# Normalising the last two chunks of V as steps of their own, behind the second pair's masks, in an attention, gMLP and GLU kernel

## The chip, the cores and the metric

The kernel runs on one core of a Trainium2 chip. The metric is the device time of one execution, in microseconds (us). Times below are from the profiler's trace of one execution unless they are called the median.

## The reference

Three blocks follow one another, for a batch of 4 sequences of 576 positions. All arrays are float32.

```python
# 1 attention: 8 heads of 64, causal, window of 128, ALiBi bias
attn = softmax(where(mask, q @ k.T / 8 + bias, -1e9));  x = heads_joined(attn @ v)
# 2 gMLP: d_model 512, d_ff 1024
h = gelu_tanh(x @ w_in);  u, v = h[..., :512], h[..., 512:]
v_n = (v - mean(v)) / sqrt(var(v) + 1e-6) * g_ln
x2 = x + (u * (einsum('ts,bsd->btd', w_sg, v_n) + b_sg)) @ w_out
# 3 GLU: width-3 convolution over positions
h2 = relu(x2 @ w_in2);  out = (h2 * sigmoid(conv3(h2, conv_w))) @ w_out2
```

The change concerns `v_n` of the first sequence (batch 0): the mean and the variance of each position's 512 values of v, and the normalised rows that the product with `w_sg` needs over all 576 positions.

## The kernel before

Every matrix product of blocks 2 and 3 is made of three float32r products (high part times high part, high times low, low times high), so every operand is split into a high and a low part: a copy that rounds (`hi`, L246) and a subtraction of it from the source (`lo`, L249).

The work is a list of steps, written out in `_steps` (L54 to L121) and run in that order by `run` (L889). A letter names the step and numbers its batch and tile. C is a head pair's scores on TensorE (PE) and its nine masked row maxima on VectorE (DVE), L451; E its nine exponentials on ScalarE (ACT), L493; N the reciprocal of the sums (L498, L499) and the nine scalings by it, on GpSimd (POOL) or DVE (L242); T its transposes; A the product with the attention's v, out of which an x tile comes. V is one chunk of 128 positions of the gMLP's v (chunk 4 has 64): 12 matmuls into `psv`, Gelu on ACT, mean and variance on DVE (L781, L782), the reciprocal root on POOL (L784, L785), the normalisation on DVE (L786) and its split, high part on ACT, low part on DVE (L787). U is one tile of u, G one of the product with `w_sg` (14 matmuls into `pss`, evicted by DVE at L843, then multiplied by u on POOL at L821 and split, which is the gate), W one of the product with `w_out` (`pso`). L and M load a pair's k, q and v; g and o load and split a piece of `w_sg` and `w_out`, the last with five DVE instructions (L324 to L331), a copy on ACT and a subtraction on POOL.

A scheduler turns the list into one fixed order for each engine: it takes instructions by readiness in a time model and, among the ready ones, by their place in the list. At run time each engine then keeps its order. `add_manual_dep` with `follow` puts one instruction behind another in that order, and adds no semaphore. All of `act`'s activations keep the list's order among themselves (L188). `pick` (L204) chooses an engine for some copies by booked loads; `book` adds to those loads.

In batch 0 the V, U, g and o steps are mixed with the scores of batch 1 (line 93 and 94 of `_steps`): V0.4 and V0.3 stand ahead of C1.1, the scores of batch 1's second pair; then come U0.1.2, U0.1.3 and C1.2, then E1.0, N1.0 and the four tiles G0.0.0 to G0.0.3. A G tile reads the normalised chunks in the order 0, 1, 2, 3, 4 (L834), three matmuls for each of the first four and two for the last. The scores have six PSUM banks (L276), and one pair takes five of them, which its masks give back.

Of the kernel before, what the change touches and what calls it, by code (L numbers as in the profile page):

```python
# [7 lines left out]
F32 = mybir.dt.float32  # L8
# [3 lines left out]
AF = mybir.ActivationFunctionType  # L12
ALU = mybir.AluOpType

B, H, S, D = 4, 8, 576, 64
P = 128
DM = H * D
FF = 1024
HF = FF // 2
# [12 lines left out]
NV = 3  # L32
# [21 lines left out]
def _steps():  # L54


    def of(p):
        return f"{p // NP}.{p % NP}"

    def scores(p):  # L60
        return [f"C{of(p)}"]

    def weigh(p):
        return [f"E{of(p)}", f"N{of(p)}"]

    def back(p):
        return [f"T{of(p)}", f"A{of(p)}"]

    def halves(p):
        return [f"X{of(p)}.0", f"X{of(p)}.1"]  # L70

    def loads(p):
        return [f"L{of(p)}", f"M{of(p)}"]

    weave = lambda main, more: [
        x for i, m in enumerate(main) for x in [m] + more[i * len(more) // len(main) : (i + 1) * len(more) // len(main)]
    ]
    put_by = [f"a{i}.{c}" for i in (1, 0) for c in range(16)]
    s = """
        l0.0 k0 l1.0 k5 l2.0 l3.0 v0.0 v1.0 v2.0 v3.0 j1.0 j1.1 l0.1  # L80
        c0.0 e0.0 c1.0 e1.0 n0.0 c2.0 e2.0 t0.0 n1.0 c3.0 e3.0 l1.1 j1.2 j1.3 v0.1 i1.0 z0.0 X0.0.0 t1.0 n2.0 z1.0 X0.1.0
        l2.1 v1.1 i1.1 t2.0 n3.0 z2.0 X0.2.0 c0.1 e0.1 l3.1 j0.0 i1.2 t3.0 z3.0 X0.3.0 c1.1 e1.1 v2.1 i1.3 n0.1 c2.1 j0.1 v3.1 j0.2 t0.1 e2.1 n1.1 z0.1
        i0.0 c3.1 e3.1 j0.3 i0.1 k4 V0.0 t1.1 n2.1 z1.1 V0.1 t2.1 n3.1 z2.1 i0.2 U0.0.0 i0.3 t3.1 z3.1 X0.0.1 U0.0.1
        X0.1.1 U0.0.2 X0.2.1 X0.3.1
    """.split()
    for b in range(B - 1):
        p = NP * (b + 1)
        V = [f"V{b}.{j}" for j in range(5)]
        U = [[f"U{b}.{half}.{m}" for m in range(4)] for half in range(2)]
        G = [[f"G{b}.{half}.{m}" for m in range(4)] for half in range(2)]  # L90
        W = [[f"W{b}.{half}.{m}" for m in range(4)] for half in range(2)]
        if b == 0:
            uv = ["g0", "g1", V[2], "g2", "o0.0", U[0][3], "g3", "o0.1", V[4]] + loads(p) + ["g4", "o1.0"] + scores(p) + ["o1.1", V[3], "o2.0", "o2.1"]
            uv += loads(p + 1) + U[1][:2] + ["o3.0"] + scores(p + 1) + ["o3.1"] + loads(p + 2) + U[1][2:] + scores(p + 2)
        else:
            uv = V[:2] + loads(p) + scores(p) + V[2:] + loads(p + 1) + scores(p + 1) + U[0] + loads(p + 2) + U[1][:1] + scores(p + 2) + U[1][1:]
        T, A = ([f"{x}{of(p + i)}" for i in range(4)] for x in "TA")
        gw = weigh(p) + G[0] + weigh(p + 1) + G[1][:1] + loads(p + 3) + T[:1] + G[1][1:2] + W[0][:1] + A[:1] + halves(p)
        gw += weigh(p + 2) + W[0][1:2] + T[1:2] + W[0][2:] + A[1:2] + scores(p + 3) + halves(p + 1) + weigh(p + 3) + T[2:3] + G[1][2:3]
        gw += A[2:3] + halves(p + 2) + G[1][3:] + T[3:] + W[1][:1] + A[3:] + halves(p + 3) + W[1][1:]  # L100
        if b == 0:
            s += uv + gw
        else:
            now = put_by[10 * b - 10 : 10 * b]
            s += ["B1"] + weave(uv, now[:4]) + ["B0"] + weave(gw, now[4:])
    first = " ".join(s)
    n = [f"V3.{j}" for j in (0, 1, 2, 4, 3)] + [f"U3.{half}.{m}" for half in range(2) for m in range(4)]
    n += [f"G3.0.{m}" for m in range(4)] + ["G3.1.0"] + [f"W3.0.{m}" for m in range(4)]
    n += [f"G3.1.{m}" for m in range(1, 4)] + [f"W3.1.{m}" for m in range(4)]

    for m in range(4):
        n[n.index(f"U3.{m % 2}.{m // 2 + 1}")] += f" w0.{m // 2}.{m % 2}"
    n[n.index("W3.0.3")] += " y0.0"
    n[n.index("G3.1.2")] += " y0.1"
    n[n.index("W3.1.0")] += " y0.2"
    n[n.index("W3.1.1")] += " y0.3"
    s = weave(n[:-6], put_by[LATE:]) + n[-6:]
    late = [f"w1.{k}.{h}" for k in range(4) for h in range(2)]
    s = s[:-6] + weave(s[-6:], late)
    second = " ".join(["x0.0.1.2.3"] + s)  # L120
    return first, second  # L121
# [13 lines left out]
def attention_gmlp_glu_kernel(  # L135
# [21 lines left out]
    nc = tc.nc  # L157
# [25 lines left out]
    def act(*args, **kw):  # L183

        book("act", (225 if "accum_out" in kw else 60) + width(args[0]))
        ins = nc.scalar.activation(*args, **kw)  # L186
        if last_act:
            tc.add_manual_dep(ins.ins, last_act[-1], follow, reason="tables")  # L188
        last_act.append(ins.ins.name)
        return ins  # L190
# [10 lines left out]
    def book(eng, ns):  # L201
        load[eng] = max(load[eng], load["pe"] - SLACK) + ns
# [6 lines left out]
    def mm(out, lhsT, rhs, start, stop, **kw):  # L209
        per = 2 if lhsT.dtype == F32 else 1  # L210
        book_pe = max(width(rhs), 2 * width(lhsT) if per == 1 else width(lhsT)) * per / 2.4
        load["pe"] += book_pe
        return nc.tensor.matmul(out, lhsT, rhs, start=start, stop=stop, **kw)  # L213

    def copy(dst, src, psum=False, engines="act dve pool"):
        n = width(src)
        cost = dict(act=52 + 0.85 * n, dve=67 + 1.04 * n) if psum else dict(
            act=20 + 1.0 * n, dve=150 + 0.52 * n, pool=130 + 0.9 * n
        )
        eng = pick({e: c for e, c in cost.items() if e in engines.split()})  # L220
        if eng == "act":
            return nc.scalar.copy(dst, src)  # L222
        if eng == "dve":
            return nc.vector.tensor_copy(dst, src)
        return nc.gpsimd.tensor_scalar(dst, src, 1.0, 1.0, op0=ALU.mult, op1=ALU.mult)
# [31 lines left out]
    mpool = p1.enter_context(tc.tile_pool(name="mpool", bufs=2))  # L257
# [491 lines left out]
    def m_v(b, j):  # L749
        ps = bank("psv")  # L750

        r = P if j < 4 else 64
        half, o = j // 2 if j < 4 else 1, j % 2 * P
        if j < 4:
            work = [(a[:, o : o + P], w, P) for k in range(NK) for hi, lo in [xg[b, k, half]] for a, w in ((hi, winh), (hi, winl), (lo, winh))]
            work = [(a, w[:, i // 3, HF:], n) for i, (a, w, n) in enumerate(work)]
        else:
            xt = [mpool.tile([P, 320], F32R, tag="t1", name="xt", bufs=NT1)[:, :P] for _ in range(NK)]
            for k in range(NK):
                copy(xt[k].rearrange("p (a n) -> p a n", a=2), xtail[b, k], engines="pool")  # L760
            work = [(xt[k], winh[:, k, HF:], P) for k in range(NK)]
            work += [(xt[k][:, :D], winl[:, k, HF:], D) for k in range(NK)]
        for n, (a, w, rows) in enumerate(work):
            mm(ps[:rows], a, w, start=n == 0, stop=n == len(work) - 1, skip_group_check=j == 4)
        if j < 4:
            vn = mpool.tile([P, 2, HF], F32R, tag="vn", name="vn", bufs=NVN)
            hi, lo = vn[:, 0, :], vn[:, 1, :]
        else:
            if b == 0:
                pad(mpool, 6, "pad1")  # L770
            hi = lo = mpool.tile([P, HF], F32R, tag="vt", name="vn", bufs=1)
        v = mpool.tile([P, HF], F32, tag="v", name="v", bufs=NV)
        if j < 4:
            act(v, ps, AF.Gelu_apprx_tanh)
        else:
            copy(v[:r], ps[r:], True, "act")
            tt(v[:r], ps[:r], v[:r], ALU.add, "dve")
            act(v[:r], v[:r], AF.Gelu_apprx_tanh)
        bs, ba, rs = small(6, "bs"), small(2, "ba"), small(1, "rs")
        book("dve", 1200)  # L780
        nc.vector.bn_stats(bs[:r], v[:r])  # L781
        nc.vector.bn_aggr(ba[:r], bs[:r])  # L782
        book("pool", 800)
        nc.gpsimd.tensor_scalar(rs[:r], ba[:r, 1:2], 1.0, 1e-6, op0=ALU.mult, op1=ALU.add)  # L784
        nc.gpsimd.tensor_tensor(rs[:r], rs[:r], mhalf[:r], op=ALU.pow)  # L785
        nc.vector.tensor_scalar(v[:r], v[:r], ba[:r, 0:1], rs[:r], op0=ALU.subtract, op1=ALU.mult)  # L786
        split(hi[:r], lo if j < 4 else hi[64:], v[:r], "vn first")  # L787
        vns[b, j] = (hi, lo)

# [82 lines left out]
    def constants(i):  # L872
# [10 lines left out]
    STEP = dict(  # L883
        B=rotations,
        k=constants, l=z_load, v=z_vload, c=z_scores, e=z_exp, n=z_norm, t=z_transpose, z=z_av, j=w_in_load, L=a_load, M=a_vload, C=a_scores, E=a_exp, N=a_norm, T=a_transpose, A=a_av,
        X=a_xsplit, V=m_v, U=m_u, G=m_sg, W=m_wo, i=w_in_piece, g=w_sg_piece, o=w_out_piece, a=w2_piece,
    )

    def run(steps):  # L889
# [229 lines left out]
```

## Time and profile before

| | |
|---|---|
| time, median of 3 runs | 542.7 us (542.19 to 546.43) |
| the profiled execution | 543.29 us, span 541.1 us |
| PE busy | 520.7 us (96%) |
| DVE busy | 367.7 us (68%) |
| ACT busy | 258.7 us (48%) |
| POOL busy | 243.2 us (45%) |
| chain that ended last | PE 62%, DVE 14%, ACT 9%, POOL 7%, DMA 5% |

Busy shares are means over stages with different limits. The change acts in the stretch from 60 to 100 us after the span's start, so the rows below are from there. In a timeline's row the columns are start and duration in us, engine, line, operation, output and input tile, shape, the number of instructions merged, and in brackets the idle time before it with what ended it. The duration of one row may reach some hundredths into the next row's start, because instructions overlap at their ends.

### The profile page before, as it was taken

The numbers are of one execution on the slowest core, as the hardware profiler recorded it, in microseconds if no ns is written. First come the engines' busy times: TensorE is split into PE (matmuls) and PEld (weight loads), VectorE is DVE, ScalarE is ACT, GpSimd is POOL, SyncE is SP. The second block draws the span as 40 slices with busy tenths as digits, with TensorE's granted clock in tenths as the row PEclk, the third lists the DMA queues.
The fourth block names the chain that finished last, engine by engine and source line by source line (L and its number), as shares of the span: only waits on it lengthen the run. The fifth ranks groups of instructions, "written<-read, shape, count | busy, mean of one in ns | idle before, by whom it ended". The sixth has DMA issues, their size and how long they took to land.

```text
span 541.1 us, 11980 instructions
## 1 busy us (share of the span) xinstructions
PE 520.7 (96%) x4548; PEld 474.7 (88%) x4548; DVE 367.7 (68%) x959; ACT 258.7 (48%) x673; POOL 243.2 (45%) x383
## 2 busy tenths in 40 slices
PE   8997989999998999999999999999999999999997
PEld 6776879898898988989988999998998999999887
DVE  4999798754878875879767688687567354654300
ACT  6694578342458451376534434452554333444310
POOL 2444238542146363246453344245586545465500
PEclk9999989999999999999999999999999999999999
DMA  8974541433261765243643433902202100100011
GB/s 290 394 241 175 150 121 52 148 113 98 89 201 37 218 187 190 82 124 92 173 144 115 155 101 131 337 13 52 75 21 81 66 22 19 42 21 27 33 39 59
DMA packets 33209, 63.93 MB, mean 118 GB/s; under 512 B 3968, under 2 KB 13952, under 8 KB 33152
## 3 DMA queue, kind: packets, MB, share of 16 engines
q1 hardware_dynamic: 33008, 63.04, 35.8%
q8 instruction: 36, 0.59, 0.5%
q14 instruction: 21, 0.17, 0.1%
q10 hardware_dynamic: 144, 0.13, 0.1%
HBM read 48.47 MB, written 14.68 MB: 117 GB/s over the span
## 4 chain that ended last, share of the span: by engine, by line
PE 62%; DVE 14%; ACT 9%; POOL 7%; DMA 5%; issue 3%; SPq 0%; ACTq 0%; DVEq 0%; POOLq 0%
PE psg L213 31%; PE psv L213 7%; PE pso L213 6%; PE psu L213 5%; PE o L213 4%; ACT t L186 3%; PE pss L213 3%; PE sc L213 3%; POOL t L242 3%; PE pT L515 2%; DMA w<-in_w_in_dram 2%; DVE t L451 1%; DVE wa L330 1%; DMA kq<-in_qk_dram 1%; DVE wa L328 1%
## 5 line engine op out<-in xcount | busy, mean ns | idle before, releaser
L213 PEld LDWEIGHTS psg<-x2g,w 128*128 128x128 f32 x768 | 103.1, 188 | 2.4 <-ACT hb L973 0.7
L213 PE MATMUL psg<-x2g,w 128*128 128x256 f32 (+1 forms) x768 | 104.6, 294 | 0.6 <-ACT hb L973 0.5
L213 PE MATMUL psg<-wout,gh 128*128 128x512 f32 (+1 forms) x272 | 80.1, 378 | 0.0
L186 ACT ACTIVATE t<-t,st 128x192 f32<-128x192 f32 (+1 forms) x144 | 61.9, 431 | 15.0 <-DVE st L451 15.0
L213 PE MATMUL pss<-wsg,vn 128*128 128x256 f32 (+1 forms) x448 | 63.6, 298 | 3.6 <-DVE t L843 3.0
L213 PEld LDWEIGHTS pss<-wsg,vn 128*128 128x128 f32 x448 | 60.5, 190 | 4.7 <-DVE t L843 4.0
L977 DVE SCALAR_TENSOR_TENSOR cc<-hb,cw,cc 128x576 f32<-128x576 f32 x32 | 26.6, 832 | 46.9 <-POOL cc L242 46.9
L213 PEld LDWEIGHTS psg<-wout,gh 128*128 128x128 f32 x272 | 49.8, 188 | 8.7
L213 PE MATMUL psu<-xg,win 128*128 128x320 f32 (+1 forms) x384 | 54.2, 298 | 2.6 <-ACT win L222 1.7
L213 PEld LDWEIGHTS psu<-xg,win 128*128 128x128 f32 x384 | 51.7, 188 | 3.7 <-ACT win L222 1.8
L213 PE MATMUL pso<-gh,wo 128*128 128x256 f32 (+1 forms) x256 | 51.8, 300 | 0.5 <-DVE t L843 0.5
L213 PE MATMUL psg<-wout,gl 128*128 128x512 f32 (+1 forms) x136 | 50.9, 378 | 0.0
L213 PE MATMUL psv<-win,xg 128*128 128x512 f32 x192 | 47.6, 398 | 0.9 <-DVE wa L328 0.9
L242 POOL TENSOR_SCALAR cc<-hb,cw 128x576 f32<-128x576 f32 x32 | 28.3, 885 | 42.7 <-ACT hb L973 42.7
L451 DVE CUSTOM_DVE_ANT_0 t<-sc,tab 128x192 f32<-128x192 f32 (+1 forms) x144 | 40.4, 335 | 5.4 <-PE sc L213 5.0
L973 ACT ACTIVATE hb<-psg 128x576 f32<-128x576 f32 x32 | 20.7, 651 | 47.5 <-PE psg L213 45.0
L213 PEld LDWEIGHTS psv<-win,xg 128*128 128x128 f32 x192 | 35.5, 188 | 8.7 <-ACT win L222 1.0
L231 DVE TENSOR_TENSOR gg<-cc,hb 128x576 f32<-128x576 f32 x32 | 30.1, 943 | 17.2 <-ACT cc L186 17.0
L213 PEld LDWEIGHTS pso<-gh,wo 128*128 128x128 f32 x256 | 40.3, 188 | 1.7 <-DVE t L843 1.2
L213 PE MATMUL pso<-gl,wo 128*128 128x256 f32 (+1 forms) x128 | 36.9, 301 | 1.3 <-POOL gl L231 0.6
L231 POOL TENSOR_TENSOR t<-t,u 128x256 f32<-128x256 f32 (+1 forms) x32 | 27.2, 854 | 18.6 <-DVE t L843 18.4
L231 POOL TENSOR_TENSOR gl<-gg,gh 128x512 fp32r<-128x512 f32 x24 | 33.7, 1404 | 0.6
(101 smaller groups left out, 960.4 us busy)
## 6 DMA issues: line engine op xcount, KB each, us to landing
V<-in_v_dram SPq DMA_DIRECT2D x12, 704.0 KB, 4.7
x2s<-x2d SPq DMA_DIRECT2D x16, 288.0 KB, 2.9
w<-in_w_in_dram SPq DMA_DIRECT2D x8, 512.0 KB, 7.5
w<-in_w_out_dram SPq DMA_DIRECT2D x16, 256.0 KB, 3.2
w<-in_w_in_dram SPq DMA_DIRECT2D x16, 256.0 KB, 2.8
wout<-w2d SPq DMA_DIRECT2D x8, 512.0 KB, 6.0
q<-in_q_dram SPq DMA_DIRECT2D x12, 320.0 KB, 4.0
out_dram<-ot SPq DMA_DIRECT2D x15, 256.0 KB, 2.0
```

What stands on the lines that cost most here:

```text
L186: ins = nc.scalar.activation(*args, **kw)
L213: return nc.tensor.matmul(out, lhsT, rhs, start=start, stop=stop, **kw)
L231: return (nc.vector if eng == "dve" else nc.gpsimd).tensor_tensor(dst, a, b, op=op)
L242: e.tensor_scalar(dst, src, col, 1.0, op0=ALU.mult, op1=ALU.mult)
L328: tc.keep_in_program_order(clamp.tensor_scalar(f(a), f(a), W_LOW, W_HIGH, op0=ALU.max, op1=ALU.min))
L330: nc.vector.scalar_tensor_tensor(a, high, 0xC0000000, a, op0=ALU.bitwise_and, op1=ALU.bitwise_or)
L451: nc.vector.tensor_tensor_reduce(e, bank, table, scale=-SCALE, scalar=3e38, op0=ALU.add, op1=ALU.min, accum_out=mx)
L515: ins = nc.tensor.transpose(ps[:, i * P : (i + 1) * P], src, ident)
L973: nc.scalar.activation(h[:, 1 : S + 1], ps[:, 256 : 256 + S], AF.Relu)
L977: nc.vector.scalar_tensor_tensor(cc, h[:, 0:S], cw[:, 0, c : c + 1], cc, op0=ALU.mult, op1=ALU.add)
```

## The change

V0.4 and V0.3 end after the variance. What is left of them (reciprocal root, normalisation, split) becomes a step `s`, and `s0.4 s0.3` stand behind C1.1 in the list. In batch 0 the normalisation of chunks 3 and 4 is also ordered behind the last mask recorded so far, which is C1.1's ninth, on the same engine. The tiles for the normalised rows are allocated in the new step. The other chunks and batches run the same instructions in the same order as before.

```diff
-            uv += loads(p + 1) + U[1][:2] + ["o3.0"] + scores(p + 1) + ["o3.1"] + loads(p + 2) + ...
+            uv += loads(p + 1) + U[1][:2] + ["o3.0"] + scores(p + 1) + ["s0.4", "s0.3", "o3.1"] + loads(p + 2) + ...
...
+        bs, ba = small(6, "bs"), small(2, "ba")
+        book("dve", 1200)
+        nc.vector.bn_stats(bs[:r], v[:r])
+        nc.vector.bn_aggr(ba[:r], bs[:r])
+        vs[b, j] = (v, ba)
+        if b or j < 3:
+            m_vnorm(b, j)
+
+    vs = {}
+
+    def m_vnorm(b, j):
+
+        v, ba = vs.pop((b, j))
+        r = P if j < 4 else 64
         if j < 4:
             vn = mpool.tile([P, 2, HF], F32R, tag="vn", name="vn", bufs=NVN)
...
-        bs, ba, rs = small(6, "bs"), small(2, "ba"), small(1, "rs")
-        book("dve", 1200)
-        nc.vector.bn_stats(bs[:r], v[:r])
-        nc.vector.bn_aggr(ba[:r], bs[:r])
+        rs = small(1, "rs")
         book("pool", 800)
         nc.gpsimd.tensor_scalar(rs[:r], ba[:r, 1:2], 1.0, 1e-6, op0=ALU.mult, op1=ALU.add)
         nc.gpsimd.tensor_tensor(rs[:r], rs[:r], mhalf[:r], op=ALU.pow)
-        nc.vector.tensor_scalar(v[:r], v[:r], ba[:r, 0:1], rs[:r], op0=ALU.subtract, op1=ALU.mult)
+        ins = nc.vector.tensor_scalar(v[:r], v[:r], ba[:r, 0:1], rs[:r], op0=ALU.subtract, op1=ALU.mult)
+        if b == 0 and j > 2:
+            tc.add_manual_dep(ins.ins, masks[0].ins.name, follow, reason="masks first")
         split(hi[:r], lo if j < 4 else hi[64:], v[:r], "vn first")
         vns[b, j] = (hi, lo)
```

## Rows read from the trace of the kernel before

**Rows 1.** Windows: us; busy PE, PEld, DVE, ACT, POOL (instructions); clock; DMA share; GB/s

```profile
68.00:76.00 8.00, 6.68 (x93) 5.97 (x92) 7.05 (x24) 4.48 (x9) 3.99 (x6) 1.00 0.37 103
76.00:82.00 6.00, 5.23 (x45) 5.14 (x46) 5.97 (x37) 6.00 (x28) 1.48 (x2) 0.72 0.55 178
82.00:90.00 8.00, 7.83 (x62) 7.42 (x61) 7.76 (x27) 7.71 (x34) 7.26 (x14) 1.00 0.15 53
90.00:99.00 9.00, 8.14 (x95) 7.00 (x93) 7.19 (x15) 3.83 (x11) 9.00 (x17) 1.00 0.26 83
```

**Rows 2.** Chain that ended last, 50 to 108 us: start, us, engine and line

```profile
82.42 0.23 DVE r L499
...
82.74 4.20 POOL t L242 x9
...
99.32 1.75 PE pso L213 x13
```

**Rows 3.** Timeline of PE, 50 to 128 us

```profile
67.98 1.98 PE L213 MATMUL sc<-k,q 64*64 64x128 f32 x46
69.66 3.81 PE L213 MATMUL psu<-xg,win 128*128 128x320 f32 x24
73.40 1.28 PE L213 MATMUL sc<-k,q 64*64 64x128 f32 x22
76.77 2.49 PE L213 MATMUL sc<-k,q 64*64 64x192 f32 x24 [2.09 <-DVE st L451]
78.80 10.24 PE L213 MATMUL pss<-wsg,vn 128*128 128x256 f32 x70
```

**Rows 4.** Timeline of DVE, 36 to 128 us

```profile
44.01 1.49 DVE L786 TENSOR_SCALAR v<-v,ba,rs 128x512 f32<-128x512 f32 x1
...
70.43 0.54 DVE L786 TENSOR_SCALAR v<-v,ba,rs 64x512 f32<-64x512 f32 x1 [0.45 <-POOL rs L785]
...
71.76 0.96 DVE L786 TENSOR_SCALAR v<-v,ba,rs 128x512 f32<-128x512 f32 x1 [0.46 <-POOL rs L785]
72.64 0.28 DVE L451 CUSTOM_DVE_ANT_0 t<-sc,tab 128x128 f32<-128x128 f32 x1
...
74.26 1.80 DVE L231 TENSOR_TENSOR vn<-v,vn 64x512 fp32r<-64x512 f32 x2
...
77.30 0.35 DVE L451 CUSTOM_DVE_ANT_0 t<-sc,tab 128x192 f32<-128x192 f32 x1
...
79.85 0.28 DVE L451 CUSTOM_DVE_ANT_0 t<-sc,tab 128x128 f32<-128x128 f32 x1
...
82.55 0.42 DVE L843 SCALAR_TENSOR_TENSOR t<-pss,gln,bsg 128x256 f32<-128x256 f32 x1
```

**Rows 5.** Timeline of ACT, 50 to 128 us

```profile
72.75 0.62 ACT L222 CAST vn<-v 128x512 fp32r<-128x512 f32 x1 [1.13 <-DVE v L786]
...
73.89 0.76 ACT L186 ACTIVATE u<-psu 128x320 f32<-128x320 f32 x2
74.66 1.28 ACT L186 ACT_TABLE_LOAD   x1
75.96 0.40 ACT L186 ACTIVATE t<-t,st 128x128 f32<-128x128 f32 x1
...
79.66 0.45 ACT L186 ACTIVATE t<-t,st 128x192 f32<-128x192 f32 x1
```

**Rows 6.** Timeline of POOL, 50 to 128 us

```profile
71.69 0.75 POOL L231 TENSOR_TENSOR wo<-wa,wo 128x256 fp32r<-128x256 f32 x1
74.06 0.76 POOL L231 TENSOR_TENSOR wo<-wa,wo 128x256 fp32r<-128x256 f32 x1 [1.62 <-ACT wo L222]
...
86.91 2.55 POOL L231 TENSOR_TENSOR t<-t,u 128x256 f32<-128x256 f32 x3
```

**Rows 7.** Windows of the `pss` instructions alone: PE, PEld, DVE, clock, DMA, GB/s

```profile
78.70:79.70 1.00, 0.90 (x4) 0.97 (x5) 0.00 (x0) 0.50 0.00 0
79.70:80.70 1.00, 1.00 (x8) 1.00 (x8) 0.00 (x0) 0.79 0.57 111
```

More of the change, by code (lines that the diff above doesn't have):

```diff
@@ L93, in _steps @@
             uv = ["g0", "g1", V[2], "g2", "o0.0", U[0][3], "g3", "o0.1", V[4]] + loads(p) + ["g4", "o1.0"] + scores(p) + ["o1.1", V[3], "o2.0", "o2.1"]
-            uv += loads(p + 1) + U[1][:2] + ["o3.0"] + scores(p + 1) + ["o3.1"] + loads(p + 2) + U[1][2:] + scores(p + 2)
+            uv += loads(p + 1) + U[1][:2] + ["o3.0"] + scores(p + 1) + ["s0.4", "s0.3", "o3.1"] + loads(p + 2) + U[1][2:] + scores(p + 2)
         else:
@@ L764, in m_v @@
             mm(ps[:rows], a, w, start=n == 0, stop=n == len(work) - 1, skip_group_check=j == 4)
+        v = mpool.tile([P, HF], F32, tag="v", name="v", bufs=NV)
+        if j < 4:
+            act(v, ps, AF.Gelu_apprx_tanh)
+        else:
+            copy(v[:r], ps[r:], True, "act")
+            tt(v[:r], ps[:r], v[:r], ALU.add, "dve")
+            act(v[:r], v[:r], AF.Gelu_apprx_tanh)
+        bs, ba = small(6, "bs"), small(2, "ba")
[9 more added lines that the diff above has]
+        r = P if j < 4 else 64
         if j < 4:
@@ L771, in m_v @@
             hi = lo = mpool.tile([P, HF], F32R, tag="vt", name="vn", bufs=1)
[L772 to L778, printed above, removed]
-        bs, ba, rs = small(6, "bs"), small(2, "ba"), small(1, "rs")
-        book("dve", 1200)
-        nc.vector.bn_stats(bs[:r], v[:r])
-        nc.vector.bn_aggr(ba[:r], bs[:r])
+        rs = small(1, "rs")
         book("pool", 800)
@@ L885, in attention_gmlp_glu_kernel @@
         k=constants, l=z_load, v=z_vload, c=z_scores, e=z_exp, n=z_norm, t=z_transpose, z=z_av, j=w_in_load, L=a_load, M=a_vload, C=a_scores, E=a_exp, N=a_norm, T=a_transpose, A=a_av,
-        X=a_xsplit, V=m_v, U=m_u, G=m_sg, W=m_wo, i=w_in_piece, g=w_sg_piece, o=w_out_piece, a=w2_piece,
+        X=a_xsplit, V=m_v, s=m_vnorm, U=m_u, G=m_sg, W=m_wo, i=w_in_piece, g=w_sg_piece, o=w_out_piece, a=w2_piece,
     )
```

## The prediction

> **What bounds the kernel now.** I read the busy shares first, then the chain of waits, then a table by stage for 60 to 100 us, then each engine's order there. Over the whole span TensorE is the bound, but a local change is worth what its stage allows. In the stage table [rows 1] VectorE works 5.97 of the 6 us from 76 to 82 and ScalarE 6.00, while GpSimd works 1.48; from 90 to 99 us GpSimd works 9.00 of 9. The chain [rows 2] says how these hang together: VectorE's work runs without a gap up to the reciprocal of the first pair's sums at 82.42; that releases GpSimd's nine scalings at 82.74, and from there GpSimd runs without a gap until the first `w_out` product can be finished at 99.32 on TensorE. After that the chain is nearly all TensorE's. So the stage ends when GpSimd ends, GpSimd's start is set by that reciprocal, and the reciprocal by whatever stands ahead of it in VectorE's order.
>
> Two things stand ahead of it that the change touches. The normalisations of chunks 4 and 3 start at 70.43 and 71.76, each after VectorE sat idle for GpSimd's reciprocal root, 0.45 and 0.46 us, and the second pair's first mask only follows at 72.64 [rows 4], though TensorE had done that pair's scores by about 69.7 [rows 3]. Both low parts of the split (1.80 us together) also lie among the masks, so the ninth mask starts at 77.30. The third pair's scores lack banks because of it: 22 matmuls go at 73.40, then TensorE idles 2.09 us for a mask and does the other 24 at 76.77 [rows 3]. After that idle time its granted clock is at its lower level (1.2 GHz, shown as 0.50), 4 of the `pss` matmuls in the first us and 8 in the next [rows 7].
>
> **The change part by part.**
>
> The normalisations no longer stand ahead of the masks. Removed are VectorE's two waits, 0.45 + 0.46 = 0.91 us: by the time the ninth mask is through, both roots are long there (the second one released VectorE at 71.76). The masks then run from about 70.0 instead of 72.64, with some 2.4 us of their own (79.85 to 82.3 for the third pair's nine [rows 4], with nothing between) and some 0.9 us of `w_out` pieces among them, and end at about 73.4. The banks are free when TensorE reaches the third pair's scores at 73.40, so the 2.09 us of idle time go, and with them the lower clock. Those are worth something to TensorE alone: 24 score matmuls took 2.03 us (76.77 to 78.80) where 46 took 1.68 (67.98 to 69.66), so 1.15 us lost, and twelve `pss` matmuls took 2 us where some 1.1 us is their full-clock time (I take 0.9 us): 2.09 + 1.15 + 0.9 = 4.1 us. I cost this at nothing in the sum, because GpSimd's chain, not TensorE, ends the stage; it is the first rival.
>
> The moved work itself is not less: two normalisations (0.54 us each when undisturbed, the row at 70.43), two high parts on ScalarE (0.62 us each [rows 5]) and two low parts (1.80 us). It still lies ahead of the reciprocal in VectorE's order, so it gives nothing but the waits.
>
> One of the two normalisations took 0.96 us, beginning just as GpSimd's `w_out` subtraction of 0.75 us did (71.69 [rows 6]), and the one at 44.01 even 1.49 us [rows 4]; so beside a GpSimd instruction one is slower by 0.42 to 0.95. At their new place, some 73.4 to 74.4, another such subtraction starts at 74.06. Bounds: both free of it (0.42 saved), or both beside one (0.42 and 0.95 more, less the 0.42 saved, so 0.95 lost). I take half of the saving, 0.21, as the subtraction can meet only the second one's end. The Trainium skill, SBUF — State Buffer, "SBUF: two separate sides", has this as an exclusive lock: a VectorE instruction that uses two ports or has two SBUF inputs and a GpSimd one hold each other out for whole instructions, which speaks against putting four such VectorE instructions anywhere near GpSimd's work. By it the estimate is one subtraction's 0.75 us for each meeting; the 0.42 at 71.76 is less than that, the 0.95 at 44.01 more, and the rows' own numbers stay in the sum.
>
> ScalarE: the two high parts leave their place at 71.0 and 72.75 (in front of U's Gelu) and come behind about 74. Their waits of about a us on the normalisation go, so the last Gelu ends at about 73.85, when its matmuls (69.66 + 3.81) are through, instead of 74.65. Then two casts of together some 1.1 us, the table load of 1.28, and the first pair's nine exponentials, from 75.96 to 80.2 before (4.25 us [rows 5]): 73.85 + 1.1 + 1.3 + 4.25 = 80.5 instead of 80.2. That is ahead of the reciprocal wherever the latter falls in this sum (81.3 or later), so this costs nothing; the cover is 0.8 us. The Trainium skill, ScalarE: Activation LUTs, "What ACT_TABLE_LOAD costs", prices a change of table set at 2.66 us with its drain, and by it the exponentials would end at 81.9 and eat the cover; here the row shows 1.28 us and the next exponential at 75.96, 0.02 us after the load, so the trace disagrees and the row decides.
>
> GpSimd: the two roots keep their inputs and can run at 69 to 71.7 as now; behind a `w_out` piece they would be 0.75 later, still before 73.4. No DMA is in the moved steps, so SyncE's queue keeps its order. TensorE's `pss` tiles begin when the third pair's scores are done, at about 73.40 + 1.68 = 75.1 instead of 78.80, and the first one is finished some 3 us sooner. Its eviction on VectorE (0.42 us, at 82.55 before, behind the reciprocal) can then come ahead of the reciprocal, and its gate (2.55 / 3 = 0.85 us [rows 6]) falls into time in which GpSimd idled. That is 0.85 - 0.42 = 0.43 us for the chain. Bounds: none (the eviction stays behind), or three gates with their evictions, 1.3 us; I take one, since the third pair's masks come ahead of it in the list.
>
> What the normalised chunks now wait for: the tenth `pss` matmul needs chunk 3. From 75.1 it is due at about 76.2; normalised at 74.4, cast by 75.5, its low part is there at about 76.5. TensorE would wait some tenths of a us, with 2 us in hand before GpSimd's chain feels it. The tiles held longer (v, mean and variance) are next written by batch 1's first chunk, far behind. The booked loads are the same in sum, and no free choice of an engine lies between the old and the new places.
>
> Sum: 0.91 + 0.21 + 0.43 = 1.55 us off the start of GpSimd's chain, hence off the first `w_out` product and off what follows, which is TensorE's own. The profiled execution took 543.29 us (span 541.1), 0.6 us above the median; 543.29 - 1.55 = 541.74 on its scale, 541.1 on the median's.
>
> **The rivals.**
>
> A: TensorE gets all of its 4.1 us, 542.7 - 4.1 = 538.6. For it: GpSimd has 4.5 idle us between 76 and 82 [rows 1] into which gates could go, if the scheduler puts the earlier evictions ahead of the masks. Against it: VectorE, which has to evict, has no time free there. Chance 0.23.
>
> B: nothing moves, 542.7, within some 0.4. VectorE's saved 0.91 goes into new meetings with GpSimd (bound 0.95 above), or the reciprocal is held where it was because the exponentials end 2 us later than my 80.5, with `w_out` casts between them. That the edge does not do what it says belongs here: it is only an order, and if the scheduler fills the room ahead of the masks with `w_out` pieces, the masks stay at 72.6. Chance 0.21.
>
> C: slower. The high parts end up behind the first pair's nine exponentials in ScalarE's order, since they are ready at the same time. They would end at 80.2 + 1.2 = 81.4, the low part at 82.1 (0.68 of it), while the twelfth `pss` matmul, the first that reads chunk 3's low part, started at about 80.7 before (4 + 8 matmuls [rows 7]). That is 1.4 us late, and TensorE, idle from 76.2 on, would come back at its lower clock, worth about 1 us as in [rows 7]: +2.4, 545.1. It decides from the point where chunk 3's low part ends after 80.7. Against it: the new steps stand ahead of the exponentials in the list. Chance 0.14.
>
> **How the numbers follow.** My forecast, 541.1, gets 0.42. Its own range by the bounds above is 540.1 (0.91 + 0.42 + 1.3 = 2.6 saved) to 542.7 (0.91 - 0.95 + 0, nothing saved). The range has to reach A and B; from 537.2, the bounds of A with the evictions ahead of time, to 544.2, which takes in B and leaves out most of C (0.12) and the lowest end of A (0.05). Between faster and slower by 1% (5.4 us, about what a measurement of this kernel can tell from no change) lie all four cases at their centres. Faster than 537.3 needs A and more behind it, 0.07; slower than 548.1 needs C and a reordering of what follows, 0.04; within, 0.89.
>
> **What would show it.** The idle time before the normalisations on VectorE gone, the second pair's ninth mask at about 73.5, no idle time in the third pair's scores and a clock of 1.00 throughout 76 to 82 us; the reciprocal's start at 81.3 (82.42 - 0.91 - 0.21) to 81.7 (with one eviction ahead of it), GpSimd still at full busy time from there to the first `w_out` product, and that at about 97.8. A GpSimd with gaps there speaks for A; chunk 3's low part behind 80.7 with a TensorE wait in the first `pss` tile for C. The prediction is wrong if the stage's gain is given back later than 100 us, or if the first `w_out` product is early by more than 3 us.

## The result and the profile after

| | before | after |
|---|---|---|
| median of 20 runs each, side by side | 544.06 us (542.01 to 547.58) | 546.73 us (545.3 to 549.14) |
| ratio | | 1.0052, 95% interval 1.0033 to 1.007 |
| the profiled execution | 543.29 us, span 541.1 | 546.27 us, span 544.1 |

The change makes the kernel 0.5% slower. The prediction was 541.1 us, 537.2 to 544.2, so the median lies above its range. It does so as a ratio too: the kernel before had 542.7 us when the forecast was made and 544.06 here, and the range reaches to 544.2 / 542.7 = 1.0028.

The page of the kernel after, its busy shares and the chain that ended last by engine:

```profile
PE 523.8 (96%) x4548; PEld 478.2 (88%) x4548; DVE 369.1 (68%) x959; ACT 258.5 (48%) x673; POOL 242.6 (45%) x383
...
PE 64%; DVE 14%; ACT 11%; POOL 4%; issue 3%; DMA 3%; SPq 0%; POOLq 0%; DVEq 0%; ACTq 0%
```

Work per engine is nearly the same. ScalarE's share of the chain rose from 9 to 11%, GpSimd's fell from 7 to 4%. In this stage the chain runs through other engines than before [rows 2]: from the normalisation through ScalarE to the reciprocal and the first eviction, and from there on TensorE (start, us, engine and line, as there):

```profile
75.44 0.46 DVE v L797
...
76.45 0.61 ACT vn L222
...
78.71 3.07 ACT t L186 x14
...
83.49 0.35 DVE t L856
...
83.89 7.06 PE pss L213 x42
```

The stage table of the kernel after, columns as in [rows 1]:

```profile
68.00:76.00 8.00, 8.00 (x121) 7.48 (x121) 7.44 (x35) 1.77 (x5) 3.80 (x6) 1.00 0.52 176
76.00:82.00 6.00, 4.27 (x26) 3.61 (x25) 5.63 (x26) 5.97 (x20) 0.00 (x0) 0.86 0.46 143
82.00:90.00 8.00, 6.15 (x38) 6.12 (x38) 6.51 (x18) 8.00 (x38) 7.14 (x13) 0.68 0.02 6
```

ScalarE works only 1.77 us of the 8 from 68 to 76, where it worked 4.48. TensorE issues 121 matmuls there instead of 93, but then only 64 from 76 to 90 instead of 107. VectorE's timeline of the kernel after shows why; the new normalisation is line 797, the eviction line 856:

```profile
69.99 0.43 DVE L330 SCALAR_TENSOR_TENSOR wa<-wst,wa 128x256 uint32<-128x256 uint32 x1
70.45 0.42 DVE L331 SCALAR_TENSOR_TENSOR wa<-wst,wa 128x256 uint32<-128x256 uint32 x1
70.79 0.28 DVE L451 CUSTOM_DVE_ANT_0 t<-sc,tab 128x128 f32<-128x128 f32 x1
...
72.30 0.81 DVE L324 TENSOR_SCALAR wa<-wst 128x256 uint32<-128x256 uint32 x1 [0.46 <-POOL wo L231]
...
75.08 0.35 DVE L451 CUSTOM_DVE_ANT_0 t<-sc,tab 128x192 f32<-128x192 f32 x1
...
81.33 0.35 DVE L451 CUSTOM_DVE_ANT_0 t<-sc,tab 128x192 f32<-128x192 f32 x1
...
82.99 0.17 DVE L498 TENSOR_SCALAR r<-st 128x9 f32<-128x9 f32 x1 [1.30 <-ACT t L186]
...
83.28 0.21 DVE L499 RECIPROCAL r<-r 128x9 f32<-128x9 f32 x1
83.41 0.42 DVE L856 SCALAR_TENSOR_TENSOR t<-pss,gln,bsg 128x256 f32<-128x256 f32 x1
```

The two waits for GpSimd's root are gone, as predicted [rows 4]. But two instructions of a `w_out` piece stand in the place that became free (69.99 and 70.45): the first of them stood between the two normalisations before, at 70.89, the second behind two masks, at 73.13. And another piece among the masks waits 0.46 us for GpSimd's subtraction to give back the `wa` buffer and then takes 0.81 us. So the ninth mask ends at 75.43, not at 73.4. The third pair's masks are nevertheless done at 81.7, 0.6 us earlier than before; only then does VectorE stand idle, 1.30 us, for the exponentials. ScalarE's timeline of the kernel after:

```profile
75.92 1.14 ACT L222 CAST vn<-v 64x512 fp32r<-64x512 f32 x2 [3.75 <-DVE v L797]
76.97 0.43 ACT L186 ACTIVATE u<-psu 128x320 f32<-128x320 f32 x1
77.41 1.28 ACT L186 ACT_TABLE_LOAD   x1
78.71 0.40 ACT L186 ACTIVATE t<-t,st 128x128 f32<-128x128 f32 x1
```

Both casts stand ahead of the last Gelu in ScalarE's order. The Gelu's matmuls are done at 73.45 (69.64 + 3.81), but it starts at 76.97, behind casts that wait 3.75 us for the late normalisation; the table load and the exponentials follow, the first at 78.71 instead of 75.96 [rows 5]. GpSimd after:

```profile
71.52 1.45 POOL L231 TENSOR_TENSOR wo<-wa,wo 128x256 fp32r<-128x256 f32 x2
82.15 0.73 POOL L231 TENSOR_TENSOR wo<-wa,wo 128x256 fp32r<-128x256 f32 x1 [9.18 <-ACT wo L222]
83.60 1.74 POOL L242 TENSOR_SCALAR t<-t,r 128x128 f32<-128x128 f32 x4 [0.71 <-DVE r L499]
85.31 0.74 POOL L231 TENSOR_TENSOR wo<-wa,wo 128x256 fp32r<-128x256 f32 x1
```

The scalings start at 83.60 instead of 82.74 [rows 2], +0.86, and in GpSimd's new order a `w_out` subtraction of 0.74 us stands between them, where before both such subtractions were done ahead of them:

```profile
79.84 1.48 POOL L231 TENSOR_TENSOR wo<-wa,wo 128x256 fp32r<-128x256 f32 x2 [5.02 <-ACT wo L222]
```

Together that is 1.60 us; from 83.60 GpSimd again runs without a gap to 100.83. TensorE after:

```profile
67.97 1.97 PE L213 MATMUL sc<-k,q 64*64 64x128 f32 x46
69.64 3.81 PE L213 MATMUL psu<-xg,win 128*128 128x320 f32 x24
73.39 2.38 PE L213 MATMUL sc<-k,q 64*64 64x128 f32 x46
75.47 1.36 PE L213 MATMUL pss<-wsg,vn 128*128 128x256 f32 x9
77.12 0.50 PE L213 MATMUL pss<-wsg,vn 128*128 128x256 f32 x2 [0.29 <-ACT vn L222]
79.05 2.99 PE L213 MATMUL pss<-wsg,vn 128*128 128x256 f32 x17 [1.43 <-DVE vn L231]
83.89 7.06 PE L213 MATMUL pss<-wsg,vn 128*128 128x256 f32 x42 [1.85 <-DVE t L856]
...
100.88 0.38 PE L213 MATMUL pso<-gl,wo 128*128 128x256 f32 x1 [0.33 <-POOL gl L231]
```

The third pair's scores run without a gap, and `pss` begins 3.3 us sooner [rows 3]. Yet TensorE waits 0.29 and 1.43 us for the two parts of chunk 3, and after two tiles (9 + 2 + 17 = 28 matmuls) for the first eviction, which stands behind the reciprocal. The first `w_out` product is finished at 100.88, 1.56 us after 99.32 [rows 2], and waits there for GpSimd. The next one starts at 101.34, where the chain has an eviction on VectorE (100.83): the path through TensorE is by now about as late as that through GpSimd.

### The profile page after: what moved, and what is told of

It reads as the page before. It is cut to its first block, busy times and chain, and to the rows that moved or that the text cites. A ratio compares the mean times of both kernels' runs of the same rounds, so it can differ in the third digit from the quotient of the medians.

```text
span 544.1 us, 11979 instructions
## 1 busy us (share of the span) xinstructions
PE 523.8 (96%) x4548; PEld 478.2 (88%) x4548; DVE 369.1 (68%) x959; ACT 258.5 (48%) x673; POOL 242.6 (45%) x383
## 4 chain that ended last, share of the span: by engine, by line
PE 64%; DVE 14%; ACT 11%; POOL 4%; issue 3%; DMA 3%; SPq 0%; POOLq 0%; DVEq 0%; ACTq 0%
PE psg L213 31%; PE psv L213 8%; PE pso L213 6%; ACT t L186 6%; PE pss L213 6%; PE psu L213 5%; PE sc L213 3%; PE o L213 3%; PE pT L515 2%; POOL t L242 1%; DVE wa L330 1%; DMA w<-in_w_in_dram 1%; DVE wa L328 1%; DVE wa L329 1%; DVE t L451 1%
## 5 line engine op out<-in xcount | busy, mean ns | idle before, releaser
L213 PE MATMUL pss<-wsg,vn 128*128 128x256 f32 (+1 forms) x448 | 67.2, 309 | 7.3 <-DVE t L856 5.6
L213 PEld LDWEIGHTS pss<-wsg,vn 128*128 128x128 f32 x448 | 63.6, 199 | 8.4 <-DVE t L856 6.3
L242 POOL TENSOR_SCALAR t<-t,r 128x192 f32<-128x192 f32 (+1 forms) x70 | 31.2, 462 | 6.5 <-DVE r L499 3.7
```

Of the source, the lines that this page charges most:

```text
L242: e.tensor_scalar(dst, src, col, 1.0, op0=ALU.mult, op1=ALU.mult)
```

## The experiments

Each ratio is to the kernel before, run beside it, with its 95% interval. Executions of one kernel spread over some 6 us, so the trace of the stage is read beside the ratio. Some profiled executions enter the stage up to 3.3 us later than others, so the times of this table, in us, are counted from the first matmul of the second pair's scores (67.98 before). In e3b_exp1 and e11_exp1_evict the matmuls of the first two products are mingled, so their times of the first product are good to about 1 us only.

| kernel | ninth mask ends | reciprocal starts | VectorE's wait for ScalarE | first `w_out` product | ratio |
|---|---|---|---|---|---|
| before | 9.67 | 14.44 | 0 | 31.34 | |
| after | 7.46 | 15.31 | 1.30 | 32.91 | 1.0052 |
| e1_pool | 7.46 | 15.17 | 0 | 32.81 | 1.0050 |
| e3b_exp1 | 7.52 | 16.52 | 0 | 33.41 | 1.0064 |
| e11_exp1_evict | 7.38 | 16.38 | 0 | 32.00 | 1.0031 |
| e15_recip | 7.40 | 15.33 | 0 | 32.28 | 1.0057 |
| e20_latecast | 7.74 | 15.51 | 1.30 | 33.33 | 1.0060 |
| e19_again | 7.41 | 13.91 | 0 | 30.89 | 0.9987 |
| e16a_masks | 5.36 | 13.57 | 0 | 30.44 | 0.9999 |
| e18_cast | 5.28 | 13.15 | 0.39 | (order differs) | 1.0001 |

**Is it the list or the edge?** e4_noedge is the kernel after without the edge behind the masks.

```diff
-        if b == 0 and j > 2:
-            tc.add_manual_dep(ins.ins, masks[0].ins.name, follow, reason="masks first")
```

> The changed kernel without the edge behind the masks: only the split of the step and its new place in the list are left. Both theories: the scheduler issues the normalisation where it stood before, each engine's order is that of the kernel before, ratio 0.999 to 1.001. If the place in the list or the held tiles cost something by themselves, 1.002 or more. Its trace also shows how much of the later stages (after 110 us) differs between two executions of one order.

544.6 us, ratio 1.0023 (0.9994 to 1.0052); every engine's order is that of the kernel before. So splitting V and its new place in the list move nothing: the edge is the change.

**The casts off ScalarE.** e1_pool is the kernel after with the two casts on GpSimd, e9_before_pool the kernel before with the same.

```diff
-        split(hi[:r], lo if j < 4 else hi[64:], v[:r], "vn first")
+        split(hi[:r], lo if j < 4 else hi[64:], v[:r], "vn late" if b == 0 and j > 2 else "vn first")   # hi: pool
```

> The changed kernel with the high parts of chunks 3 and 4 cast on GpSimd instead of ScalarE; nothing else is edited. Theory A (ScalarE's order: both casts stand ahead of the last Gelu and of the exponentials' table load, and wait for the late normalisation): first exponential near 75.2 us instead of 78.7, the ninth done near 79.5, the reciprocal no longer waits for ScalarE and starts near 81.7, first G tiles evicted 1.5 us sooner; ratio to the kernel before 0.996 to 1.001. Theory B (VectorE: the masks are held by w_out pieces that wait for GpSimd, and everything behind is late): masks as late as in the changed kernel (ninth near 75.1), ratio 1.004 to 1.006. A wrong in part: the two casts on GpSimd meet VectorE's work and give some 0.6 us back.

> The kernel before with the high parts of chunks 3 and 4 cast on GpSimd; nothing else. Theory A: ScalarE's two waits for the normalisation (0.79 and 1.13 us) are gone there too, the last Gelu ends near 73.9 instead of 74.65 and the exponentials start 0.75 us sooner, ratio 0.997 to 1.000. Theory B: no gain, or a small loss through GpSimd meeting VectorE, ratio 1.000 to 1.002.

e1_pool: 547.14 us, 1.005 (1.0022 to 1.0077). e9_before_pool: 545.13, 1.0016 (0.9987 to 1.0045). The wait for ScalarE is gone, yet the time is not, because VectorE's work meets GpSimd's. VectorE's timeline in e1_pool, then GpSimd's:

```profile
76.63 0.70 DVE L329 TENSOR_SCALAR wa<-wa 128x256 uint32<-128x256 uint32 x1
77.36 0.98 DVE L231 TENSOR_TENSOR vn<-v,vn 64x512 fp32r<-64x512 f32 x1
...
79.65 0.96 DVE L331 SCALAR_TENSOR_TENSOR wa<-wst,wa 128x256 uint32<-128x256 uint32 x1
...
82.90 0.16 DVE L498 TENSOR_SCALAR r<-st 128x9 f32<-128x9 f32 x1
```

```profile
76.00 1.79 POOL L225 TENSOR_SCALAR vn<-v 64x512 fp32r<-64x512 f32 x2 [3.01 <-DVE v L797]
79.31 1.02 POOL L231 TENSOR_TENSOR wo<-wa,wo 128x256 fp32r<-128x256 f32 x1 [1.52 <-ACT wo L222]
...
85.20 0.74 POOL L231 TENSOR_TENSOR wo<-wa,wo 128x256 fp32r<-128x256 f32 x1
```

Three instructions that take 0.29, 0.69 and 0.42 us elsewhere take 0.70, 0.98 and 0.96, 1.24 us more, and VectorE reaches the sums at 82.90 by itself. The first two lie beside the casts, the third beside a `w_out` subtraction that came at 82.15 in the kernel after. The second subtraction still stands among the scalings (85.20), though its cast was done at 81.05: GpSimd's order has it there. With the reciprocal 0.73 us late the two make up the 1.47 us by which the first product is late. TensorE's clock was 1.00 from 80 to 88 us in this run, and the first product no earlier than in the kernel after, so the lower clock that the kernel after shows there is not what makes it late.

**The `w_out` pieces behind the masks, the casts behind the first exponential.** e5_pieces moves four `w_out` steps behind the normalisations in the list and orders two of them behind the masks; e3b_exp1 orders the casts behind ScalarE's first exponential; e14_pieces_exp1 does both; e11_exp1_evict is e3b_exp1 with the last piece behind the eviction of G0.1.0.

```diff
 # e5_pieces
-... scores(p) + ["o1.1", V[3], "o2.0", "o2.1"] ... + ["o3.0"] + scores(p + 1) + ["s0.4", "s0.3", "o3.1"]
+... scores(p) + [V[3]] ... + scores(p + 1) + ["s0.4", "s0.3", "o1.1", "o2.0", "o2.1", "o3.0", "o3.1"]
 # e3b_exp1
+            for x in late:     # the two casts
+                tc.add_manual_dep(x, ins.ins.name, follow, reason="exponentials first")
```

> The changed kernel with the two w_out pieces that stood among the second pair's masks (o1.1, o2.0) put behind them, in the list and by the same kind of edge; the casts stay on ScalarE. Theory B: ninth mask near 73.3 instead of 75.1 and the whole loss is gone, ratio 0.996 to 1.000. Theory A: normalisation and casts come 2 us sooner, so the first exponential near 76.7, still 0.7 us later than before; ratio 1.000 to 1.003.

> The changed kernel with both casts of the high part ordered behind the first of the pair's exponentials, still on ScalarE, so that they no longer stand ahead of the last Gelu and of the table load. Theory A (that order is the cause): first exponential near 75.3 us, casts at 76 to 77, the ninth exponential done near 81.2, the reciprocal not waiting for ScalarE, GpSimd's nine scalings from about 82 instead of 83.6, the first w_out tile done near 99 instead of 100.9; ratio to the kernel before 0.997 to 1.001. Theory B (VectorE's masks, late for the w_out pieces): unchanged masks, so the stage stays 1.5 us or more late, ratio 1.003 to 1.006.

> Both repairs together: casts behind the first exponential, and the w_out pieces o1.1 and o2.0 behind the second pair's masks. Theory A and B both: ninth mask near 73.3, ninth exponential near 80.6, reciprocal near 81. What the late pieces give back: with them behind the masks alone the first w_out tile was 1.6 us early and the tiles after it 2 to 3 us late, so here too the gain should be gone by 120 us; ratio 0.999 to 1.004. If the late pieces are no cost, 0.994 to 0.998.

> The casts behind the first exponential, and the last w_out piece on VectorE behind the eviction of the first G tile of the second half, which it stood ahead of in every kernel so far. If that order is the next bound of the stage (VectorE waits there for GpSimd's subtraction, 1.7 to 1.8 us, with the eviction ready), the tiles of the first half end about 1 us sooner than in the kernel with the first repair alone: ratio 0.996 to 0.999. If GpSimd's low parts of the gates bound it, the same as that kernel.

546.54 us, 1.0041 (1.0013 to 1.0068); 547.56, 1.0064 (1.0037 to 1.009); 546.32, 1.0039 (1.0007 to 1.0071); 545.58, 1.0031 (1.0004 to 1.0059). The ratios of e5_pieces and e3b_exp1 lie outside what either theory expected, and that of e11_exp1_evict between its two. e5_pieces has its first product about 1.6 us sooner than before, counted as in the table, but is 4.6 us late at the first `pss` matmul after it, e14_pieces_exp1 4.8: the pieces that were pushed back are now late. e3b_exp1 and e11_exp1_evict have no wait for ScalarE, but the scheduler drew `w_out` work and an eviction in between the sums and their reciprocal. Each of these mends one wait and makes another, so none of them decides.

**The change itself again**, to see its own spread.

> The changed kernel once more, for its floor and a second trace: stage to 108 us again 1.9 us late. If the 0.9 us more that the medians show is made by the change in later stages, they show again in the same places (168 and 245 us); if it is a matter of where TensorE's clock happens to be lower in an execution, they move or vanish.

545.79 us, 1.0035 (1.0011 to 1.006), 1.9 us above the kernel before. In its profile the same stage takes 33.21 us to the first product, +1.87.

**One edit between two kernels.** e15_recip is e11_exp1_evict with the reciprocal ahead of the first eviction and of one `w_out` piece; e16a_masks is e15_recip with the one piece that stood among the second pair's masks behind the ninth of them; e12_before_evict is the kernel before with the edge on the last piece that both have.

```diff
 # e15_recip: on VectorE, behind the reciprocal of N1.0
+            for x in soon:     # the first instruction of w_out piece 3.0; G0.0.0's eviction likewise
+                tc.add_manual_dep(x, ins.ins.name, follow, reason="reciprocal first")
 # e16a_masks, besides
+            for x in piece:    # the first instruction of w_out piece 1.1
+                tc.add_manual_dep(x, masks[0].ins.name, follow, reason="masks first")
```

> The changed kernel, the two casts behind ScalarE's first exponential, the first pair's reciprocal ahead of the first eviction and of one w_out piece on VectorE, the last w_out piece behind the eviction of G0.1.0. Theory (the stage ends with GpSimd, whose start the reciprocal sets, and the w_out piece among the masks is still there): the reciprocal at about 83.1 us (82.42 before), the scalings from 83.4, the first w_out product at about 99.9 (+0.6), time +0.5 to +1 us, ratio 1.001 to 1.002. Rival (TensorE's waits in pieces and the lower clock after them set the loss): the first w_out product again 1.5 to 2 us late although the reciprocal is early, ratio 1.003 to 1.005.

> As e15_recip, and the one w_out piece that stood among the second pair's masks behind the ninth of them. Theory (both failed steps mended: masks end early, exponentials early, nothing between them and the reciprocal but 0.3 us): ninth mask at about 73.2 us, reciprocal at about 81.0, scalings from 81.3, the first w_out product at about 97.9, 1.4 us ahead of the kernel before; ratio 0.997 to 0.998 if it is kept. Rival (the room is taken by the w_out pieces, which then come late for the second group of products): the first product early, but nothing left of it by 120 us, ratio 1.000 to 1.004.

> The kernel before, with only the last w_out piece ordered behind the eviction of G0.1.0 on VectorE, which the two others have too. Theory: its wait (1.7 us at 93.6) moves behind that eviction, the chain of GpSimd is the same, so within 0.5 us of the kernel before, ratio 0.999 to 1.001. If it is faster by more, what the other two gain is this edit's and not that of the change.

547.43 us, 1.0057 (1.0029 to 1.0086); 544.65, 0.9999 (0.9977 to 1.0022); 544.11, 0.9993 (0.996 to 1.0026). With that one edge the loss is gone, and the intervals do not overlap; a repeat of e16a_masks, further below, came out at 1.0018 (0.9995 to 1.0041), and that interval does overlap the one of e15_recip. The ratio of e15_recip lies above both its theory and its rival: the reciprocal came when forecast, but the second product waited 1.40 us for an eviction at 101.82. VectorE in e15_recip, then in e16a_masks:

```profile
72.13 0.82 DVE L324 TENSOR_SCALAR wa<-wst 128x256 uint32<-128x256 uint32 x1 [0.45 <-POOL wo L231]
...
82.73 0.17 DVE L506 TENSOR_SCALAR r<-st 128x9 f32<-128x9 f32 x1
...
83.19 0.21 DVE L507 RECIPROCAL r<-r 128x9 f32<-128x9 f32 x1
```

```profile
72.75 0.35 DVE L453 CUSTOM_DVE_ANT_0 t<-sc,tab 128x192 f32<-128x192 f32 x1
...
81.31 0.21 DVE L507 RECIPROCAL r<-r 128x9 f32<-128x9 f32 x1
```

The ninth mask ends at 73.1 and the reciprocal starts at 81.31, close to the prediction's own numbers (73.4, 81.3). What is left of the gain is seen on TensorE in e16a_masks:

```profile
98.18 0.39 PE L213 MATMUL pso<-gl,wo 128*128 128x256 f32 x1 [0.31 <-POOL gl L231]
...
99.04 0.51 PE L213 MATMUL pso<-gh,wo 128*128 128x256 f32 x2 [0.48 <-DVE t L876]
```

Counted from where the stage begins, the reciprocal is 0.87 us early and the first product 0.90. But the next tile waits 0.48 us for an eviction on VectorE, and at the first `pss` matmul of the second group (107.21; 107.60 before) 0.15 us is left.

**Are the casts harmless, then?** e18_cast is e16a_masks with the casts where the change puts them, ahead of the Gelu.

```diff
-            tc.add_manual_dep(x, ins.ins.name, follow, reason="exponentials first")   # x: the casts
```

> As e16a_masks, but the two casts stand where the change puts them, ahead of the last Gelu in ScalarE's order. Theory (the casts ahead of the Gelu and the table load cost of themselves): the masks end at about 73.2 as in e16a_masks, the casts 74.4 to 75.5, table load at about 75.9, the nine exponentials 77.2 to 81.5 (75.0 to 80.1 in e16a_masks), so VectorE waits about 0.5 us for ScalarE and the reciprocal is at about 81.9 instead of 81.3; with the two w_out subtractions that then fall between the scalings GpSimd's chain ends 1.5 to 2 us later than in e16a_masks, ratio about 1.003. Rival (only the w_out piece among the masks mattered): no wait of VectorE for ScalarE, the chain as in e16a_masks within 0.5 us, ratio 1.000.

543.79 us, 1.0001 (0.9973 to 1.0028): the theory's ratio fails. ScalarE in e18_cast:

```profile
73.89 1.14 ACT L222 CAST vn<-v 64x512 fp32r<-64x512 f32 x2 [1.97 <-DVE v L803]
74.93 0.43 ACT L186 ACTIVATE u<-psu 128x320 f32<-128x320 f32 x1
...
76.67 0.40 ACT L186 ACTIVATE t<-t,st 128x128 f32<-128x128 f32 x1
```

The casts still stand ahead, but the normalisation is early, so the first exponential comes at 76.67. VectorE waits 0.39 us and has the reciprocal at 80.86. Not all of the theory fails: two `w_out` subtractions now stand in GpSimd's chain (83.54 and 86.26), and at the first `pss` matmul of the second group e18_cast is 0.92 us behind e16a_masks and 0.77 behind the kernel before (40.39 us from where the stage begins, 39.47 and 39.62). So with the masks early the casts ahead cost at most some 0.9 us, which a ratio with this interval can't tell from nothing.

**Late masks, with and without the casts ahead.** e19_late is e15_recip with `w_out` piece 2.1 too behind the reciprocal, so that nothing is drawn in ahead of it; e20_latecast is e19_late with the casts ahead of the Gelu; e16a_again repeats e16a_masks beside them, and e19_again repeats e19_late.

```diff
 # e19_late
-... soon if (k, half) == (3, 0) else None
+... soon if (k, half) in ((2, 1), (3, 0)) else None
```

> As e15_recip (masks late because of the w_out piece among them, casts behind the first exponential), but the next w_out piece too is held behind the reciprocal, so that nothing is drawn in ahead of it. Theory 1 (late masks cost only by what they make late behind them in other orders: ScalarE's exponentials, or w_out work drawn in): ninth mask ends at about 75.2 as in e15_recip, third pair's masks at about 81.5, no wait for ScalarE, reciprocal at about 81.8 (83.2 in e15_recip), first w_out product at about 98.8, ratio about 1.000. Theory 2 (late masks cost of themselves, by TensorE's waits for chunks 4 and 3): reciprocal early, but the first products late by over 1 us, ratio 1.003 or more.

> As e19_late, but with the casts where the change puts them, ahead of the last Gelu: the change itself with only the order at the reciprocal and the last w_out piece mended. Theory 1: ScalarE idles until about 75.8, casts to 77.0, exponentials 78.6 to 82.8, VectorE waits 1.2 us for them, reciprocal at about 83.1, first w_out product at 100.2 to 100.8, ratio 1.003 to 1.005. Rival (the late exponentials are not what costs): as e19_late.

> e16a_masks again, beside the two others: ratio 0.998 to 1.002, reciprocal at about 81.3 and first w_out product at about 98.2.

> e19_late again, to see whether it beats the kernel before. Theory: its stage costs what that of the kernel before costs (first w_out product within 0.1 us of it, counted from where the stage begins), so ratio 0.999 to 1.001. Rival: the 0.9984 of its first measurement is a gain, ratio 0.996 to 0.9985.

543.08 us, 0.9984 (0.996 to 1.0008); 546.47, 1.006 (1.0027 to 1.0093); 545.53, 1.0018 (0.9995 to 1.0041); e19_again 543.29, 0.9987 (0.9957 to 1.0017). Late masks alone cost nothing that shows; with the casts ahead they cost 0.6%. The sums on VectorE in e19_again, then in e20_latecast (which entered the stage 2.45 us later):

```profile
81.75 0.17 DVE L506 TENSOR_SCALAR r<-st 128x9 f32<-128x9 f32 x1
81.95 0.21 DVE L507 RECIPROCAL r<-r 128x9 f32<-128x9 f32 x1
```

```profile
85.73 0.17 DVE L500 TENSOR_SCALAR r<-st 128x9 f32<-128x9 f32 x1 [1.30 <-ACT t L186]
85.94 0.22 DVE L501 RECIPROCAL r<-r 128x9 f32<-128x9 f32 x1
```

The wait of 1.30 us is that of the kernel after, to the hundredth, and the first product is 2.4 us later than in e19_again: 1.60 at the reciprocal, and most of the rest in a `w_out` subtraction of 0.74 that stands among the scalings in e20_latecast (88.70) and ahead of them in e19_again. No version is shown to beat the kernel before: both measurements of e19_late hold 1 in their interval.

## Why the prediction was wrong

**The step that failed is ScalarE's**: "Then two casts of together some 1.1 us, the table load of 1.28, and the first pair's nine exponentials [...] 80.5 instead of 80.2 [...] so this costs nothing; the cover is 0.8 us." It put the Gelu first and let the casts be ready behind it. The order has the casts ahead of the Gelu, so all that follows on ScalarE hangs on the normalisation; and the normalisation came 2.0 us later than assumed. The exponentials ended at 82.9, just ahead of the sums at 82.99: 2.4 us late against a cover of 0.8. e19_late against e20_latecast shows that this is what costs, e18_cast that it needs the late normalisation: with an early one nothing shows in the ratio, and at most some 0.9 us in the trace. Nearly half of the cost was in no term of the sum: the reciprocal was 0.86 us late, and the other 0.74 is the `w_out` subtraction that the scheduler put among GpSimd's scalings.

**The size behind it** is the term "some 0.9 us of `w_out` pieces among them, and end at about 73.4". The masks began at 70.79, not 70.0 (+0.79: two instructions ahead of them, of which the one at 70.89 before had been left out of the sum and the other was drawn forward); the pieces among them took 1.68 us, not 0.9 (+0.78, of which 0.53 is the row of 0.81 against the 0.28 of its kind); and one waited 0.46. That is 2.03 of 2.03 us. Rival B had named all of it, the exponentials "2 us later than my 80.5", the room filled ahead of the masks and new meetings with GpSimd, but as reasons why nothing would move; together they lost more than the 0.91 us gained. The Trainium skill, SBUF — State Buffer, "SBUF: two separate sides", has the two engines hold each other out for whole instructions: the row at 72.30 agrees in the main, as most of its 0.81 us lies beside GpSimd's two subtractions and it ends at 73.11, 0.14 us after them (71.52 + 1.45).

**Right:** the two waits of 0.91 us and the gap in the third pair's scores went; the first product still follows the reciprocal through GpSimd's chain, and where the reciprocal came near the forecast's time (e16a_masks, 81.31, 0.87 us early), the first product was 0.90 us early. The two normalisations took 0.99 us together, with GpSimd idle beside them, against 0.54 + 0.96 before, so the term of 0.21 was if anything too small. **Also wrong:** the gate moved ahead (0.43 us). The first eviction stays behind the reciprocal in the kernel after, and where it came ahead of it (e3b_exp1, e11_exp1_evict) the reciprocal was at 84.1. TensorE's wait for chunk 3 was 0.29 + 1.43 us, not some tenths; e19_again has 0.29 + 1.57 and no loss, so it cost nothing here. The lower clock did not go, it came later (80 to 86 us), which e1_pool shows to be no part of the loss. And 0.90 us at the first product did not become 0.90 us of time, because an eviction on VectorE came late next.

**Rival A** (TensorE keeps its 4.1 us) fails much as the prediction argued, on VectorE, which has to evict: after two `pss` tiles TensorE needs an eviction, and that waits behind the reciprocal (1.85 us after, 1.90 and 2.25 in e16a_masks and e18_cast).

**Rival C** had the right sign with the mirror image of the mechanism: the casts were not too late behind the exponentials, the exponentials were too late behind the casts. Its condition was not met (chunk 3's low part was there at 78.99, not after 80.7), so that its +2.4 us come near the measured 2.7 is luck.

The Trainium skill, ScalarE: Activation LUTs, "What ACT_TABLE_LOAD costs", puts the price of a table change at 2.66 us, of which 1.28 are the load and 1.38 a drain: the load took 1.28 us again, and the exponential followed 0.02 us later (77.41, 78.71), so the rows agree on the load and show no drain.

**Open:** the stage explains +1.6 to +1.9 us; the medians differ by 2.7, those of the repeat by 1.9, and the first interval reaches down to 1.8, so it is not shown that there is a rest. In the profile after, the granted clock is also lower at 169 to 172 and 247 to 251 us. In after_again it is 1.00 from 108 to 300 us, and e4_noedge, which has the order of the kernel before, has 0.50 from 168 to 170, so those stretches go with the execution more than with the change.

## What to carry to other kernels

When work is moved on one engine, look up where its consumers stand in the other engines' orders: an instruction that waits there holds everything behind it, ready or not, and here that was a Gelu, a table load and nine exponentials. A place that becomes free in a scheduled order may be refilled, as here; price the filler, and the wait that it may bring, before the gain. A new order on one engine can also reorder another: look for work that has moved into the chain behind it. Where two delays cost mainly together, undoing either one alone shows it, provided nothing else is drawn into the gap: several kernels here mended one wait and made another.

## What the runs showed of the hardware

The stretches at the lower clock differ from execution to execution of one program. Windows of TensorE's work in the kernel after (us; busy PE, PEld; clock; DMA share; GB/s):

```profile
80.00:82.00 2.00, 2.00 (x12) 1.74 (x10) 0.57 0.90 319
...
84.00:86.00 2.00, 2.00 (x10) 2.00 (x11) 0.50 0.00 0
...
169.00:171.00 2.00, 1.85 (x8) 1.45 (x6) 0.51 0.04 8
```

In after_again, the same program, the last of these windows has a clock of 1.00. In e1_pool, which has TensorE waiting in the same places before and between the `pss` tiles, the first two have 1.00 as well. Idle time of TensorE comes before each such stretch here (1.43, 1.86 and 1.86 us), but not each idle time is followed by one (1.01, 1.43 and 1.72 us in e1_pool).
